# A decode layer on one core: half of the query's weights loaded first, w2 in six pieces, x and the result in four transfers each

## The chip, the cores and the metric

The kernel runs on one core of one Trainium2 chip. The metric is the device time in microseconds (us) of one execution, as the median of several. TensorE is called PE, VectorE DVE, ScalarE ACT, GpSimd POOL, and SyncE SP. SP computes nothing here: it only issues transfers. ACT issues a few as well.

## What is computed

One token for each of four sequences (B = 4, D = 1024) goes through an attention block with a sliding window over a cache and then through a gated feed-forward block, each with a layer norm ahead and a residual sum behind. The weights and the caches are bf16.

```python
x  = A_x                                              # [4, 1, 1024]
q  = layernorm(x) @ wq                                # wq [1024, 4096]: 32 heads of 128
k, v = k_cache[:, :, -2048:, :], v_cache[:, :, -2048:, :]   # 4 kv heads, 8 query heads to each
o  = softmax(q @ k.T * 128**-0.5) @ v
h  = x + o @ wo                                       # wo [4096, 1024]
n  = layernorm(h)
out = h + (silu(n @ w1) * (n @ w3)) @ w2              # w1, w3 [1024, 3584]; w2 [3584, 1024]
```

## The kernel before

**The ring of loads.** Everything large passes through five slots of 128 partitions x 16384 bf16 (4 MB each), in the order of the list `ring`: the K cache in two slots of two sequences each (`k`), the first half of wq, two slots without a load that hold the transposed K (`kT`), the second half of wq, V in two slots, wo in two, w1 in two, w3 in two, w2 in two. `fill()` walks the list. It takes a slot and issues its load on SP (L133), and it stops at an entry whose slot is still held; `done(name, i)`, called in the program behind the last reader of a part, goes on with it. So all large loads stand in one queue, SP's, in the ring's order, and what can hold a load back is the release of a slot by PE.

**w2 in pieces.** w2 lies as 28 rows of 1024 values in each of the 128 partitions, 256 KB for one row over all partitions. `W2B = [16, 8, 2, 2]` cuts the rows into four transfers; the first fills one slot, the other three share the next. PE takes four matmuls for a row (L491, `y2_ps`), and it waits at the head of each piece for that piece.

**x and the result.** The 4 x 1024 values of x are laid into the tile `x_nat` [128, 256] as four quarters of 256 columns: quarter c of sequence b goes to partition 32c + 8b (`S = 8`), the other partitions are zero. This is one transfer of 16 rows of 512 bytes, issued by ACT (L149). The layer norm (`layernorm_T`) reads every eighth column of the transposed tile and writes every eighth of `n_T`, and PE's operand of 32 columns has its four live ones there. The result lies the same way in `res`, and leaves in two transfers of eight rows each, one from SP (L503) and one from ACT (L504).

**The order of the work.** The order on each engine is that of the program (`manual_schedule`). PE: the sums of the first layer norm (L198); 256 transposes of K (L241), which DVE and ACT copy into `kT` by turns (L243, L245); 64 matmuls of the query (L259), 32 for each half of wq; then for each sequence the scores, the softmax and the output (L294 to L386); the projection with wo (L434); w1 and w3 (L458); w2 (L491). DVE adds the residual to the last sum (L501), and the result is sent.

**Completion.** A transfer signals its end on one of eight semaphores, which are given out in turn to all transfers, of SP and ACT alike. A transfer that takes a semaphore again waits at its issue for the one that had it before.

Of the kernel before, what the change touches and what calls it, by code (L numbers as in the profile page):

```python
# [10 lines left out]
P = 128  # L11
ACT = mybir.ActivationFunctionType
ALU = mybir.AluOpType
AX = mybir.AxisListType
BF16 = mybir.dt.bfloat16
FP32 = mybir.dt.float32
# [7 lines left out]
def kernel(  # L24
# [20 lines left out]
    nc = tc.nc  # L45

    B, _, D = A_x.shape
    Hkv, Sk, Dh = A_k_cache.shape[1], A_k_cache.shape[2], A_k_cache.shape[3]
    NQ = A_wq.shape[1]
    Hq = NQ // Dh  # L50
    REP = Hq // Hkv
    W = min(4096, max(256, Sk // 4))
    F = B_w1.shape[1]
    KC = D // P
    FC = F // P
    NK = W // P
    C = 4
    R = 32
    S = R // B
    DQ = D // C  # L60
    FQ = F // C
    FH = FQ // 2
# [5 lines left out]
    x_flat = A_x.flatten_outer_dims()  # L68
    out_flat = out.flatten_outer_dims()
# [7 lines left out]
    w1_v = B_w1.rearrange("(p kc) f -> p kc f", kc=KC)  # L77
    w3_v = B_w3.rearrange("(p kc) f -> p kc f", kc=KC)
# [7 lines left out]
    ps = ctx.enter_context(tc.tile_pool(name="ps", bufs=1, space=bass.MemoryType.PSUM))  # L86
# [3 lines left out]
    def of_cache(cache, b):  # L90
        return cache[b, :, Sk - W : Sk, :].rearrange("g (i j) d -> i g (j d)", j=JR)

    def pair(parts):
        return [parts[0:2], parts[2:4]]

    k_, v_ = (
        pair([(name, b, [JR, Dh], of_cache(cache, b)) for b in range(B)])
        for name, cache in (("k", A_k_cache), ("v", A_v_cache))
    )
    kT_ = pair([("kT", b, [JR, P], None) for b in range(B)])  # L100
    wo_ = pair([("wo", g, [1, T * D], wo_v[:, g : g + 1, :]) for g in range(Hkv)])

    def four_rows(name, view, n):
        return [[(name, i, [4, n], view[:, 4 * i : 4 * i + 4, :])] for i in range(KC // 4)]

    wq_ = four_rows("wq", wq_v, NQ)
    ring = k_ + wq_[:1] + kT_ + wq_[1:] + v_ + wo_ + four_rows("w1", w1_v, F) + four_rows("w3", w3_v, F)
    W2B = [16, 8, 2, 2]
    w2_ = []
    f0 = 0  # L110
    for i, n in enumerate(W2B):
        w2_.append(("w2", i, [n, D], w2_v[:, f0 : f0 + n, :]))
        f0 += n
    ring += [w2_[:1], w2_[1:]]
    views = {}
    taken = []
    used = set()
# [19 lines left out]
    def get(name, i):  # L137
        return views[(name, i)]

    def done(name, i):  # L140
        used.add((name, i))
        fill()
# [3 lines left out]

    x_nat = act.tile([P, DQ], BF16)
    nc.vector.memset(x_nat[:], 0.0)
    nc.scalar.dma_start(out=x_nat[::S, :], in_=x_flat.rearrange("b (c n) -> c b n", c=C))  # L149
    fill()  # L150

    ident = const.tile([P, P], BF16)
# [8 lines left out]
        out=t32[:], in_=ident[:].rearrange("p (q h) -> p h q", q=C), axis=AX.X, op=ALU.add  # L161
# [4 lines left out]
    for q in range(C):  # L166
# [3 lines left out]
        out=negm[:], in_=t32[:].rearrange("p (g r) -> p g r", g=Hkv), axis=AX.X, op=ALU.add  # L170
    )
    nc.vector.tensor_scalar(
        out=negm[:], in0=negm[:], scalar1=-1.0, scalar2=-NEG, op0=ALU.add, op1=ALU.mult
# [3 lines left out]
        out=jmask[:, :, 0], in_=ident[:].rearrange("p (j h) -> p j h", j=JM), axis=AX.X, op=ALU.add  # L177
# [6 lines left out]
    for l in range(2):  # L184
        nc.gpsimd.tensor_copy(
            out=strip[:, l, B - 1 :].rearrange("p (c x) -> p c x", c=C)[:, :, : B * Hkv].rearrange(
                "p c (g b) -> p c g b", b=B
            )[:, :, :, 0],
            in_=t32[:].rearrange("p (g c l) -> p l c g", g=Hkv, c=C)[:, l],
        )  # L190

    def layernorm_T(h_T, tag):

        both = act.tile([P, 2, KC, B], FP32, tag=tag + "_both")
        nc.vector.tensor_copy(out=both[:, 0], in_=h_T[:, :, ::S])
        nc.vector.tensor_tensor(out=both[:, 1], in0=both[:, 0], in1=both[:, 0], op=ALU.mult)  # L196
        sums_ps = ps.tile([P, 2, KC, B], FP32, tag="kt3")
        nc.tensor.matmul(sums_ps[:], lhsT=ones_f[:], rhs=both[:], start=True, stop=True)  # L198
        sums = act.tile([P, 2, B], FP32, tag=tag + "_sums")
        nc.vector.tensor_reduce(  # L200
            out=sums[:], in_=sums_ps[:].rearrange("p t k b -> p t b k"), axis=AX.X, op=ALU.add
        )
        mean = act.tile([P, 2, B], FP32, tag=tag + "_mean")
        nc.vector.tensor_single_scalar(out=mean[:], in_=sums[:], scalar=1.0 / D, op=ALU.mult)
        rstd = act.tile([P, 1, B], FP32, tag=tag + "_rstd")
        nc.vector.tensor_tensor(out=rstd[:, 0], in0=mean[:, 0], in1=mean[:, 0], op=ALU.mult)
        nc.vector.tensor_tensor(out=rstd[:, 0], in0=mean[:, 1], in1=rstd[:, 0], op=ALU.subtract)  # L207
        nc.scalar.activation(  # L208
            out=rstd[:, 0], in_=rstd[:, 0], func=ACT.Sqrt, bias=eps_t[:], scale=1.0
        )  # L210
        nc.vector.reciprocal(out=rstd[:, 0], in_=rstd[:, 0])
        n_T = act.tile([P, KC, R], BF16, tag=tag + "_nT")
        nc.gpsimd.memset(n_T[:], 0.0)
        hc = act.tile([P, KC, B], FP32, tag=tag + "_hc")
        nc.vector.tensor_tensor(
            out=hc[:], in0=both[:, 0], in1=mean[:, 0:1, :].to_broadcast([P, KC, B]), op=ALU.subtract
        )
        nc.vector.tensor_tensor(
            out=n_T[:, :, ::S], in0=hc[:], in1=rstd[:].to_broadcast([P, KC, B]), op=ALU.mult
        )  # L220
        return n_T

    def transpose_quads(dst, src, n):

        nc.vector.transpose(
            out=dst.rearrange("p j r -> p (j r)"), in_=src.rearrange("p (q j) -> p j q", j=n)
        )

    x_T = act.tile([P, KC, R], BF16)
    transpose_quads(x_T[:], x_nat[:], KC)  # L230
    xn_T = layernorm_T(x_T[:], "ln1")


    n_step = 0
# [11 lines left out]
            n_step += 1  # L246
        done("k", b)


    q_ps = [ps.tile([P, REP // 2, Dh], FP32, tag=f"sc{hf}", name=f"q_ps{hf}") for hf in range(2)]  # L250
    HALF = REP // 2
    for i in range(KC // 4):
        w = get("wq", i)
        for kk in range(4):
            kc = 4 * i + kk
            for hf in range(2):
                for c in range(C):
                    o = (2 * c + hf) * HALF * Dh
                    nc.tensor.matmul(  # L259
                        q_ps[hf][R * c : R * c + R],  # L260
                        lhsT=xn_T[:, kc, :],
                        rhs=w[:, kk, o : o + HALF * Dh],
                        start=(kc == 0),
                        stop=(kc == KC - 1),
                        tile_position=(0, R * c),
                    )
        done("wq", i)
    q_sb = act.tile([P, REP, Dh], BF16)
    nc.vector.tensor_copy(out=q_sb[:, :HALF], in_=q_ps[0][:])  # L269
    nc.scalar.copy(out=q_sb[:, HALF:], in_=q_ps[1][:])  # L270
    qT_ps = ps.tile([P, REP, Hkv, R], BF16, tag="kt0")
# [6 lines left out]
    for b in range(B):  # L278
        nc.vector.tensor_copy(  # L279
            out=Qm[:, b].rearrange("p (g y) -> p g y", y=QW)[:, :, :REP],  # L280
            in_=qT_ps[:, :, :, S * b].rearrange("p r g -> p g r"),
        )


# [122 lines left out]
    for l in range(2):  # L407
        for b in range(B):
            nc.tensor.matmul(  # L409
                on_ps[:, l],  # L410
                lhsT=strip[:, l, B - 1 - b : B - 1 - b + P],
                rhs=om[:, b],
                start=(b == 0),
                stop=(b == B - 1),
# [5 lines left out]
    oP = act.tile([P, Hkv, T, R], BF16)  # L420
    nc.gpsimd.memset(oP[:], 0.0)
    nc.vector.tensor_copy(  # L422
        out=oP[:, :, :, ::S],
        in_=oX[:, :, : Hkv * B].rearrange("p t (g b) -> p g t b", b=B),
    )

# [2 lines left out]
    for g in range(Hkv):  # L429
        w = get("wo", g)  # L430
        for t in range(T):
            for c in range(C):
                o = t * D + c * DQ
                nc.tensor.matmul(  # L434
                    y_ps[R * c : R * c + R, :],
                    lhsT=oP[:, g, t, :],
                    rhs=w[:, 0, o : o + DQ],
                    start=(g == 0 and t == 0),
                    stop=(g == Hkv - 1 and t == T - 1),
                    tile_position=(0, R * c),  # L440
# [4 lines left out]
    h_T = act.tile([P, KC, R], FP32)  # L445
    transpose_quads(h_T[:], h1[:], KC)
    hn_T = layernorm_T(h_T[:], "ln2")


# [36 lines left out]
    fc = 0  # L486
    for i, n in enumerate(W2B):
        w = get("w2", i)
        for ff in range(n):
            for c in range(C):  # L490
                nc.tensor.matmul(  # L491
                    y2_ps[R * c : R * c + R, :],
                    lhsT=hg_T[:, fc, :],
                    rhs=w[:, ff, c * DQ : (c + 1) * DQ],
                    start=(fc == 0),
                    stop=(fc == FC - 1),
                    tile_position=(0, R * c),
                )
            fc += 1
    res = act.tile([P, DQ], BF16)  # L500
    nc.vector.tensor_tensor(out=res[:], in0=y2_ps[:], in1=h1[:], op=ALU.add)  # L501
    out_v = out_flat.rearrange("b (c n) -> c b n", c=C)
    nc.sync.dma_start(out=out_v[: C // 2], in_=res[: P // 2 : S, :])  # L503
    nc.scalar.dma_start(out=out_v[C // 2 :], in_=res[P // 2 :: S, :])  # L504


# [28 lines left out]
```

## Time and profile before

| | us |
|---|---|
| median of 3 runs (lowest to highest) | 140.11 (139.94 to 140.18) |
| the profiled execution | 140.13 |
| its span in the profile | 138.3 |
| time outside the span | 1.8 |

| engine | busy us | share of the span |
|---|---|---|
| PE | 80.2 | 58% |
| DVE | 52.9 | 38% |
| ACT | 42.7 | 31% |
| queue q1 (SP's loads): 55.58 MB | | 94.4% of 16 DMA engines |

The page gives busy shares in 40 slices of the span, the DMA engines' rate beside them, and the chain of waits that ended last. The timeline lists instructions in order of time, merged, with the idle time of the engine ahead of them in brackets and what ended it; a line of a transfer in it shows the issue on the queue (SPq, ACTq), not the data. Every time below is counted from the start of the span.

### The profile page before, as it was taken

The numbers are of one execution on the slowest core, as the hardware profiler recorded it, in microseconds if no ns is written. First come the engines' busy times: TensorE is split into PE (matmuls) and PEld (weight loads), VectorE is DVE, ScalarE is ACT, GpSimd is POOL, SyncE is SP. The second block draws the span as 40 slices with busy tenths as digits, with TensorE's granted clock in tenths as the row PEclk, the third lists the DMA queues.
The fourth block names the chain that finished last, engine by engine and source line by source line (L and its number), as shares of the span: only waits on it lengthen the run. The fifth ranks groups of instructions, "written<-read, shape, count | busy, mean of one in ns | idle before, by whom it ended". The sixth has DMA issues, their size and how long they took to land.

```text
span 138.3 us, 2012 instructions
## 1 busy us (share of the span) xinstructions
PE 80.2 (58%) x866; PEld 47.5 (34%) x868; DVE 52.9 (38%) x97; ACT 42.7 (31%) x57; POOL 4.2 (3%) x18
## 2 busy tenths in 40 slices
PE   0029898921903889328918998659539901703780
PEld 0029887820301322014304434537324400202550
DVE  3036676520000235177087197540330298350001
ACT  3005988850000325998807900000040200000000
POOL 7400000000000000000000000000000000000000
PEclk9999999998555799975797799965865896555555
DMA  4999999999989999999999999999999999999930
GB/s 152 399 423 431 431 436 455 455 441 398 445 384 426 441 417 417 450 407 431 450 400 431 433 469 431 394 448 448 419 398 448 456 411 430 445 407 398 406 148 2
DMA packets 3217, 55.72 MB, mean 403 GB/s; under 512 B 360, under 2 KB 392, under 8 KB 648
## 3 DMA queue, kind: packets, MB, share of 16 engines
q1 hardware_dynamic: 3178, 55.58, 94.4%
q8 instruction: 7, 0.11, 0.3%
q10 hardware_dynamic: 30, 0.01, 0.0%
q14 instruction: 2, 0.02, 0.0%
HBM read 55.58 MB, written 0.01 MB: 402 GB/s over the span
## 4 chain that ended last, share of the span: by engine, by line
DMA 49%; PE 27%; DVE 13%; ACT 4%; SPq 3%; issue 2%; DVEq 0%
DMA s_wq<-in_A_wq_dram 29%; DMA s_w<-in_B_w_dram 20%; PE o_ps L369 10%; PE y_ps L434 5%; ACT P L334 4%; PE sc_ps L294 3%; DVE PT L346 3%; SPq L133 3%; PE gu_ps L458 2%; PE q_ps L259 2%; DVE om L386 2%; DVE od L378 2%; PE on_ps L409 1%; PE tot_ps L355 1%; PE nm_ps L323 1%
## 5 line engine op out<-in xcount | busy, mean ns | idle before, releaser
L334 ACT ACTIVATE P<-sc_ps,bias 128x512 bf16<-128x512 f32 x16 | 19.7, 1417 | 9.6 <-DVE bias L331 9.6
L241 PE MATMUL kt_ps<-ident,s_k 128*128 128x128 bf16 x256 | 17.3, 228 | 1.3 <-ACT s_kT L245 1.0
L369 PE MATMUL o_ps<-s_v,PT 128*128 128x512 bf16 x62 | 17.5, 439 | 0.3 <-issue 0.2
L241 PEld LDWEIGHTS <-s_k 128*128 128x128 bf16 x256 | 16.3, 103 | 2.3 <-issue 1.7
L245 ACT COPY s_kT<-kt_ps 128x1024 bf16<-128x1024 bf16 x16 | 15.7, 1012 | 2.5 <-PE kt_ps L241 2.5
L458 PE MATMUL gu_ps<-s_w,n_T 128*32 128x448 bf16 x128 | 10.7, 513 | 8.8 <-DMA s_w<-in_B_w_dram 6.8
L259 PE MATMUL q_ps<-s_wq,n_T 128*32 128x512 bf16 x64 | 7.0, 615 | 11.8 <-DMA s_wq<-in_A_wq_dram 11.8
L243 DVE COPY s_kT<-kt_ps 128x1024 bf16<-128x1024 bf16 x16 | 11.1, 693 | 5.8 <-PE kt_ps L241 5.8
L491 PE MATMUL y_ps<-s_w,hg_T 128*32 128x256 bf16 x112 | 6.6, 418 | 8.0 <-DMA s_w<-in_B_w_dram 8.0
L369 PEld LDWEIGHTS <-PT 128*128 128x128 bf16 x64 | 7.2, 117 | 9.2 <-issue 4.4
L346 DVE STREAM_TRANSPOSE PT<-P 128x2048 bf16<-128x2048 bf16 x4 | 9.2, 2303 | 2.7 <-ACT P L334 2.7
L208 ACT ACTIVATE rstd<-rstd,eps_t 128x4 f32<-128x4 f32 x2 | 0.6, 297 | 29.5 <-DVE rstd L207 29.5
L458 PEld LDWEIGHTS <-n_T 128*32 128x32 bf16 x128 | 4.7, 131 | 14.1 <-issue 11.6
L294 PE MATMUL sc_ps<-s_kT,Qm 128*32 128x512 bf16 x64 | 8.5, 603 | 0.4 <-DVE Qm L279 0.4
L491 PEld LDWEIGHTS <-hg_T 128*32 128x32 bf16 x112 | 4.9, 142 | 10.0 <-issue 5.9
L259 PEld LDWEIGHTS <-n_T 128*32 128x32 bf16 x64 | 2.7, 137 | 15.6 <-issue 15.5
L269 DVE CAST q_sb<-q_ps 128x512 bf16<-128x512 f32 x1 | 0.7, 692 | 18.3 <-PE q_ps L259 18.3
L198 PE MATMUL sums_ps<-both,ones_f 128*128 128x64 f32 x4 | 1.1, 373 | 11.2 <-DVE both L196 11.2
L434 PE MATMUL y_ps<-s_wo,oP 128*32 128x256 bf16 x128 | 6.5, 397 | 1.7 <-DVE oP L422 1.7
L378 DVE SCALAR_TENSOR_TENSOR od<-o_ps,rinv,jmask 128x512 f32<-128x512 f32 x4 | 3.0, 751 | 8.4 <-PE o_ps L369 8.3
L270 ACT CAST q_sb<-q_ps 128x512 bf16<-128x512 f32 x1 | 0.6, 585 | 17.8 <-PE q_ps L259 17.8
L310 PE MATMUL mx_ps<-ident_f,rmax 128*1 128x128 f32 x8 | 1.7, 302 | 7.4 <-DVE rmax L308 7.4
(68 smaller groups left out, 64.7 us busy)
## 6 DMA issues: line engine op xcount, KB each, us to landing
s_w<-in_B_w_dram SPq DMA_DIRECT2D x4, 3584.0 KB, 21.2
s_k<-in_A_k_cache_dram SPq DMA_DIRECT2D x4, 2048.0 KB, 16.1
s_wq<-in_A_wq_dram SPq DMA_DIRECT2D x2, 4096.0 KB, 35.3
s_v<-in_A_v_cache_dram SPq DMA_DIRECT2D x4, 2048.0 KB, 25.1
s_wo<-in_A_wo_dram SPq DMA_DIRECT2D x4, 2048.0 KB, 25.5
s_w<-in_B_w_dram SPq DMA_DIRECT2D x1, 4096.0 KB, 28.0
s_w<-in_B_w_dram SPq DMA_DIRECT2D x1, 2048.0 KB, 25.7
s_w<-in_B_w_dram SPq DMA_DIRECT2D x2, 512.0 KB, 27.0
```

Of the source, the lines that this page charges most:

```text
L241: nc.tensor.transpose(out=kt_ps[:, jj], in_=k[:, jb * JB + jj, :], identity=ident[:])
L243: nc.vector.tensor_copy(out=kT[:, jb * JB : (jb + 1) * JB], in_=kt_ps[:])
L245: nc.scalar.copy(out=kT[:, jb * JB : (jb + 1) * JB], in_=kt_ps[:])
L259: nc.tensor.matmul(q_ps[hf][R * c : R * c + R], lhsT=xn_T[:, kc, :], rhs=w[:, kk, o : o + HALF * Dh], start=(kc == 0), stop=(kc == KC - 1) ...
L294: nc.tensor.matmul(sc_ps[b][R * q : R * q + R], lhsT=Qm[:, b, g * R : (g + 1) * R], rhs=v[:, g, q], start=(g == 0), stop=(g == Hkv - 1), t ...
L334: nc.scalar.activation(out=P4[:, :, :, g], in_=sc_ps[b][:].rearrange("p (j i) -> p j i", i=L5), func=ACT.Exp, bias=bias[:, g : g + 1], sca ...
L346: nc.vector.transpose(out=PT[:].rearrange("p j h -> p (j h)"), in_=stage.pop(("P4", b))[:].rearrange("p j i g -> p (j i g)"),)
L369: nc.tensor.matmul(o_ps[:], lhsT=PT[:, i * JM : (i + 1) * JM, :].rearrange("p j h -> p (j h)"), rhs=v[:, i * JM : (i + 1) * JM, :], start= ...
L378: nc.vector.scalar_tensor_tensor(out=od[:], in0=o_ps[:], scalar=rinv[:, 0:1], in1=jmask[:].to_broadcast([P, JM, Dh]), op0=ALU.mult, op1=AL ...
L434: nc.tensor.matmul(y_ps[R * c : R * c + R, :], lhsT=oP[:, g, t, :], rhs=w[:, 0, o : o + DQ], start=(g == 0 and t == 0), stop=(g == Hkv - 1 ...
L458: nc.tensor.matmul(out_ps[hf][R * c : R * c + R], lhsT=hn_T[:, kc, :], rhs=w[:, kk, o : o + FH], start=(kc == 0), stop=(kc == KC - 1), til ...
L491: nc.tensor.matmul(y2_ps[R * c : R * c + R, :], lhsT=hg_T[:, fc, :], rhs=w[:, ff, c * DQ : (c + 1) * DQ], start=(fc == 0), stop=(fc == FC ...
```

## The change

The ring begins with the first half of wq and the K cache follows it; the matmuls of that half are moved in PE's program ahead of the transposes of K, and those of the second half stay behind them. w2 is cut in 7, 6, 8, 4, 2 and 1 rows, the first two in one slot, the other four in the next. Quarter c of sequence b now lies in partition 32c + b, so x arrives in four transfers of four consecutive partitions, all issued by ACT, and the result leaves in four: two from SP, two from ACT. Every tile that followed the stride of eight follows the new places (`:B` for `::S`).

```diff
-    ring = k_ + wq_[:1] + kT_ + wq_[1:] + v_ + wo_ + ...
-    W2B = [16, 8, 2, 2]
+    ring = wq_[:1] + k_ + kT_ + wq_[1:] + v_ + wo_ + ...
+    W2B = [7, 6, 8, 4, 2, 1]
...
-    ring += [w2_[:1], w2_[1:]]
+    ring += [w2_[:2], w2_[2:]]
...
-    nc.scalar.dma_start(out=x_nat[::S, :], in_=x_flat.rearrange("b (c n) -> c b n", c=C))
+    for c in range(C):
+        nc.scalar.dma_start(out=x_nat[R * c : R * c + B, :], in_=x_flat[:, c * DQ : (c + 1) * DQ])
     fill()
...
-        nc.vector.tensor_copy(out=both[:, 0], in_=h_T[:, :, ::S])
+        nc.vector.tensor_copy(out=both[:, 0], in_=h_T[:, :, :B])
...
-            out=n_T[:, :, ::S], in0=hc[:], in1=rstd[:].to_broadcast([P, KC, B]), op=ALU.mult
+            out=n_T[:, :, :B], in0=hc[:], in1=rstd[:].to_broadcast([P, KC, B]), op=ALU.mult
...
+    query(0)                      # the 32 matmuls of the first half of wq
     for b in range(B):            # the transposes of K, unchanged
...
+    query(1)                      # the 32 matmuls of the second half
...
-            in_=qT_ps[:, :, :, S * b].rearrange("p r g -> p g r"),
+            in_=qT_ps[:, :, :, b].rearrange("p r g -> p g r"),
...
-        out=oP[:, :, :, ::S],
+        out=oP[:, :, :, :B],
...
-    out_v = out_flat.rearrange("b (c n) -> c b n", c=C)
-    nc.sync.dma_start(out=out_v[: C // 2], in_=res[: P // 2 : S, :])
-    nc.scalar.dma_start(out=out_v[C // 2 :], in_=res[P // 2 :: S, :])
+    for i in range(2):
+        for half, eng in enumerate((nc.sync, nc.scalar)):
+            c = 2 * half + i
+            eng.dma_start(
+                out=out_flat[:, c * DQ : (c + 1) * DQ], in_=res[R * c : R * c + B, :]
+            )
```

More of the change, by code (lines that the diff above doesn't have):

```diff
@@ L58 @@
     R = 32
-    S = R // B
     DQ = D // C
@@ L106 @@
     wq_ = four_rows("wq", wq_v, NQ)
-    ring = k_ + wq_[:1] + kT_ + wq_[1:] + v_ + wo_ + four_rows("w1", w1_v, F) + four_rows("w3", w3_v, F)
-    W2B = [16, 8, 2, 2]
+    ring = wq_[:1] + k_ + kT_ + wq_[1:] + v_ + wo_ + four_rows("w1", w1_v, F) + four_rows("w3", w3_v, F)
+    W2B = [7, 6, 8, 4, 2, 1]
     w2_ = []
@@ L231, with query @@
     xn_T = layernorm_T(x_T[:], "ln1")
-    n_step = 0
-    for b in range(B):
-        k = get("k", b)
-        kT = get("kT", b)
-        for jb in range(JR // JB):
-            kt_ps = ps.tile([P, JB, P], BF16, tag=f"kt{n_step % 3}")
-            for jj in range(JB):
-                nc.tensor.transpose(out=kt_ps[:, jj], in_=k[:, jb * JB + jj, :], identity=ident[:])
-            if n_step % 2 == 0:
-                nc.vector.tensor_copy(out=kT[:, jb * JB : (jb + 1) * JB], in_=kt_ps[:])
-            else:
-                nc.scalar.copy(out=kT[:, jb * JB : (jb + 1) * JB], in_=kt_ps[:])
-            n_step += 1
-        done("k", b)
     q_ps = [ps.tile([P, REP // 2, Dh], FP32, tag=f"sc{hf}", name=f"q_ps{hf}") for hf in range(2)]
     HALF = REP // 2
-    for i in range(KC // 4):
+    def query(i):
         w = get("wq", i)
@@ L267 @@
         done("wq", i)
+    query(0)
+    n_step = 0
+    for b in range(B):
+        k = get("k", b)
+        kT = get("kT", b)
+        for jb in range(JR // JB):
+            kt_ps = ps.tile([P, JB, P], BF16, tag=f"kt{n_step % 3}")
+            for jj in range(JB):
+                nc.tensor.transpose(out=kt_ps[:, jj], in_=k[:, jb * JB + jj, :], identity=ident[:])
+            if n_step % 2 == 0:
+                nc.vector.tensor_copy(out=kT[:, jb * JB : (jb + 1) * JB], in_=kt_ps[:])
+            else:
+                nc.scalar.copy(out=kT[:, jb * JB : (jb + 1) * JB], in_=kt_ps[:])
+            n_step += 1
+        done("k", b)
+    query(1)
     q_sb = act.tile([P, REP, Dh], BF16)
```

## The prediction

> **What bounds the kernel now.** I read the page's slices first, then its chain.
>
> ```profile
> DMA  4999999999989999999999999999999999999930
> GB/s 152 399 423 431 431 436 455 455 441 398 445 384 426 441 417 417 450 407 431 450 400 431 433 469 431 394 448 448 419 398 448 456 411 430 445 407 398 406 148 2
> ...
> DMA 49%; PE 27%; DVE 13%; ACT 4%; SPq 3%; issue 2%; DVEq 0%
> ```
>
> The 16 DMA engines are at nine tenths or more from the second slice to the 37th, with one eight. 55.58 MB at some 430 GB/s is 129 us of the 138.3. The chain does name PE and DVE for 40%, but only because it walks back from one load's issue through the slot that let it go; the engines' row shows that the data never ran dry meanwhile. So the kernel is one stream of loads with a head and a tail, and an edit counts if it moves the first packet, the bytes' rate, the tail, or lets the queue run empty.
>
> The timeline of the last 12 us is the tail:
>
> ```profile
> 126.88 3.61 PE L491 MATMUL y_ps<-s_w,hg_T 128*32 128x256 bf16 x64 [6.53 <-DMA s_w<-in_B_w_dram]
> ...
> 131.77 2.33 PE L491 MATMUL y_ps<-s_w,hg_T 128*32 128x256 bf16 x40 [1.28 <-DMA s_w<-in_B_w_dram]
> ...
> 134.30 0.62 PE L491 MATMUL y_ps<-s_w,hg_T 128*32 128x256 bf16 x8 [0.20 <-DMA s_w<-in_B_w_dram]
> ...
> 134.97 0.42 DVE L501 TENSOR_TENSOR res<-y_ps,h 128x256 bf16<-128x256 f32 x1 [12.06 <-PE y_ps L491]
> 135.42 0.66 SPq L503 DMA_DIRECT2D out_dram<-res  x1
> 135.42 0.60 ACTq L504 DMA_DIRECT2D out_dram<-res  x1
> ```
>
> PE waits for each piece of w2: the 16 rows at 126.88, the next 8 at 131.77, the last two at 134.30. Eight matmuls, the sum and the result's way out follow. By the records of SP, its wait for the result ends at 137.43, 1.35 after its issue ends at 136.08; two further waits of 0.06 and the closing steps of all engines lead to 138.3.
>
> The timeline of the start, with the SP queue's and ACT's first issues and the end of the query:
>
> ```profile
> 0.73 2.59 SPq L133 DMA_DIRECT2D s_k<-in_A_k_cache_dram  x4
> ...
> 1.03 1.19 ACTq L149 DMA_DIRECT2D x_nat<-in_A_x_dram  x1
> ...
> 3.36 1.14 SPq L133 DMA_DIRECT2D s_wq<-in_A_wq_dram  x2
> ...
> 8.37 0.62 DVE L225 STREAM_TRANSPOSE x_T<-x_nat 128x256 bf16<-128x256 bf16 x1 [6.03 <-DMA x_nat<-in_A_x_dram]
> ...
> 28.54 10.44 SPq L133 DMA_DIRECT2D s_v<-in_A_v_cache_dram  x4
> 34.15 3.60 PE L259 MATMUL q_ps<-s_wq,n_T 128*32 128x512 bf16 x32 [5.64 <-DMA s_wq<-in_A_wq_dram]
> ...
> 43.86 3.40 PE L259 MATMUL q_ps<-s_wq,n_T 128*32 128x512 bf16 x32 [6.11 <-DMA s_wq<-in_A_wq_dram]
> ```
>
> **The new order at the start** is worth nothing in itself: either way 16.8 MB must land before the last 32 query matmuls, and half of them are already done then. What changes is PE's order, so I follow what PE now waits for. x: its 16 rows go in between the packets of the big loads; the packet records show them at 5.59, 6.22, 6.93 and 7.56 on four DMA engines, one behind each 16 KB packet of K (0.61 us), the first after five of those. Behind 32 KB packets (1.22 us) I expect the first near 8.7 and the last near 12.4; that the four issues on ACT take longer than the one of 1.19 is inside this, and ACT has nothing else queued but a table load. From x's transpose to `n_T` takes 8.37 to 12.09, 3.7 us, so n_T is ready near 16.7, behind the 4 MB of wq (two K loads had landed at 13.2). The 32 matmuls take 3.4 to 3.6: 20.3. Then 64 transposes for each sequence at some 4.5 us, behind K's landings at 18.1, 24.3, 29 and 34.1: done at about 38.7. The second half of wq lands at 43.8, so PE has 5 us in hand and the rest of PE's program starts as before.
>
> Queues it is moved past: on SP, K now stands behind wq, and the stream is the same length. The four x transfers use up completion semaphores, so in the built program the fourth K load waits for the first wq load (about 13.2) and the second wq load for the first x; three K loads are queued then, enough until about 27. V's first load needs two sequences transposed, near 29 (28.54 before), and its second pair all four, near 38.7 (37.79); at both times the queue holds more than 5 us. Later issues come 12 us or more ahead of need: the last of w1's loads is issued at 79.16, when the data ahead of it lasts until 91.6. DVE's edits of stride (0.20 to 0.46 us each) hide there too. Cost: 0; if the cover goes, one us for each us of an empty queue.
>
> The head: the first issue, of K, takes 0.65 and the first packet moves at 2.16. The wq issues at the same stage take 0.63 and 0.47, and later weights 0.33, so the gain lies between 0 and 0.33. I take **-0.1**, by the nearest rows, those of wq.
>
> **w2 in six pieces.** Two pieces more, each 8 packets for a DMA engine. From 126.88 to 131.77 eight rows in one piece took 4.89, or 0.611 a row; from 131.77 to 134.30 four rows in two pieces took 2.53, or 0.633. That is 0.06 per added piece. The packet records say 161 ns for 4 KB and 614 for 16 KB, so a packet has some 10 ns that don't scale, 0.08 a piece. Two pieces: 0.11 to 0.19 (no gain is possible, the bytes are the same); I take **+0.15**. PE's side: four matmuls a row at 58 ns each (2.33 us for 40), 0.23, against 0.61 for the row's data, so PE has caught up at the last row.
>
> The Trainium skill speaks against this: "DMA: Bandwidth & Descriptors", section on bandwidth, advises batches of 1 MiB or more and gives 341 GB/s for 1 MB against 425 for 16 MB. By an estimate from that, the 1.8 MB of the last three pieces would take 5.4 us instead of 4.3, and the sum would be 1 us longer. The trace disagrees as far as it goes: its two 0.5 MB pieces, issued long ahead, came at 414 GB/s.
>
> **The last matmuls.** Eight become four. One takes 0.37 to 0.42, four run side by side, and eight took 0.62; four need some 0.40, so **-0.2** (between -0.15 and 4 x 58 ns = -0.23).
>
> **The result.** Two issues in a row on each queue where there was one. No trace row has a transfer of four rows. Issues of 128 regular rows take 0.33 alone; those of 8 rows here 0.66 and 0.60; that of 16 rows (x) 1.19. A line through the last two gives 0.3 to 0.4 for four rows. I take 0.40: 2 x 0.40 + 0.06 between them - 0.66 = +0.20. Bounds: 2 x 0.33 + 0.05 - 0.66 = +0.05, and 2 x 0.66 + 0.06 - 0.66 = +0.72. The write itself: eight packets stood in two chains of four, 0.12 from first to last; four consecutive partitions against four rows should use four engines with one packet each, -0.09. The closing waits: the last transfer's semaphore is now the last in SP's list, so up to 0.12 of the two waits behind it lies ahead; half, -0.06. Together **+0.05** (-0.16 to +0.72).
>
> The same page, in the section on why a completion counts 16, states that a transfer uses the largest number of engines up to 16 that divides the outer size on both sides. The rows agree for the old shapes (16 against 4: four engines; 8 against 2: two). By it the new ones use four; no row shows that yet.
>
> **Sum:** -0.1 + 0.15 - 0.2 + 0.05 = -0.1. From the profiled execution's 140.13, which is the median of 140.11 within 0.02, that gives 140.0. All low ends: -0.33 + 0.11 - 0.23 - 0.16 = -0.6; all high ends: 0 + 0.19 - 0.15 + 0.72 = +0.8. One more unknown has no term: the 16 engines land a piece up to 2 us apart (132.24 to 134.26 for the last), since a few were held up by 16 KB fetches of instructions of about 1 us, and the end waits for the slowest. Another start may draw this by 0.3 either way.
>
> **Rivals.**
> 1. *Head and spread pay.* The first issue costs 0.33, the result's issues 0.33, and the slow engines come 0.3 earlier: 139.4 to 139.7. For: all later weight issues of wq's form cost 0.33. Against: the first ones cost 0.47 and 0.63.
> 2. *The result's second issue costs full price (slower).* At 0.6 to 0.66 each, the second transfer ends 0.6 to 0.7 later; with the rest, 140.45. It decides above 0.5 per issue. For: eight rows cost no less than 128 rows did, so the price may not follow the rows. Against: x, with twice the rows, cost twice.
> 3. *x comes late and blocks PE (slower).* PE's transposes now stand behind the query, which stands behind the layer norm. Up to a query that ends at 26 nothing moves; if V's first load can't be issued before 43.8, the queue runs dry, which needs the query to end past 35, x past 27. Then each us costs a us: 141 to 144. For: x is interleaved with packets of twice the length. Against: it has four packets per engine, and wq only eight.
>
> **How the numbers follow.** What a measurement of this kernel can tell from no change is 0.2%, 0.28 us. The forecast, 139.75 to 140.4, has 0.44: 0.09 of it faster, 0.32 same, 0.03 slower. Rival 1 has 0.27 (0.24 faster, 0.03 same), rival 2 has 0.25 (0.05 same, 0.20 slower), rival 3 has 0.04. So faster 0.33, same 0.40, slower 0.27. The range 139.4 to 140.8 leaves out rival 3 and the outer ends of the others.
>
> **What would show it.** Right: DMA slices at nine to the end, the first packet near 2.05, x's transpose near 13, the second query matmuls at 43 to 44, one wait of PE for each w2 piece and the last block of four matmuls at 0.4, each result issue near 0.4. Wrong: a slice of seven or less between 20 and 50 us (rival 3), result issues at 0.6 (rival 2), a last w2 landing earlier or later than 134.2 by more than 0.4 (the spread).

## The result and the profile after

The changed kernel takes 139.38 us (139.21 to 139.47, 6 runs) where the kernel before takes 139.98 (139.88 to 140.18, 6 runs beside it): a ratio of 0.9954, interval 0.9941 to 0.9967. It is faster by 0.6 us. The forecast was 140.0 in a range of 139.4 to 140.8: the stream and its cover went as told, and the head and the way of the result out were both priced too dear.

The page's slices and chain of the changed kernel:

```profile
DMA  5998999999899999999999999999999999999950
GB/s 152 458 459 382 429 434 434 415 438 505 376 410 429 415 438 419 434 429 415 443 417 429 422 467 425 438 417 434 425 430 425 425 447 388 414 437 431 400 219 2
...
DMA 51%; PE 28%; DVE 13%; ACT 4%; issue 2%; SPq 1%; DVEq 0%
```

The stream is as full as before; no slice runs dry. The timeline of its last 14 us:

```profile
124.80 1.47 PE L496 MATMUL y_ps<-s_w,hg_T 128*32 128x256 bf16 x24 [1.06 <-DMA s_w<-in_B_w_dram]
...
129.69 1.90 PE L496 MATMUL y_ps<-s_w,hg_T 128*32 128x256 bf16 x32 [3.43 <-DMA s_w<-in_B_w_dram]
...
132.19 1.04 PE L496 MATMUL y_ps<-s_w,hg_T 128*32 128x256 bf16 x16 [0.60 <-DMA s_w<-in_B_w_dram]
...
133.42 1.05 PE L496 MATMUL y_ps<-s_w,hg_T 128*32 128x256 bf16 x12 [0.18 <-DMA s_w<-in_B_w_dram]
...
134.52 0.42 DVE L506 TENSOR_TENSOR res<-y_ps,h 128x256 bf16<-128x256 f32 x1 [11.96 <-PE y_ps L496]
134.97 0.67 SPq L510 DMA_DIRECT2D out_dram<-res  x2
134.98 0.62 ACTq L510 DMA_DIRECT2D out_dram<-res  x2
```

PE finds each piece of w2 just landed and is done with it before the next; the line with 12 matmuls is the last two pieces, of two rows and of one. The last two lines hold the surprise: two issues on each queue now take 0.67 and 0.62 together, as long as one took before. The rows by tile say it for each issue (ns, smallest, median and largest; before it was 664 on SP and 599 on ACT):

```profile
L510 SPq DMA_DIRECT2D out_dram<-res x2: 274/311/348, 135.0 to 135.4; - x2
L510 ACTq DMA_DIRECT2D out_dram<-res x2: 275/292/308, 135.0 to 135.3; - x2
```

At the start, the first load's issue takes 0.65 before and 0.41 after (a line of the chain of waits before, and one of the timeline after):

```profile
0.73 0.65 SPq L133
```

```profile
0.73 0.41 SPq L132 DMA_DIRECT2D s_wq<-in_A_wq_dram  x1
```

The windows give the bytes by the time at which their packets begin (the last column is GB/s). Before, nothing moves ahead of 2.0:

```profile
1.50:2.00 0.50, 0.00 (x0) 0.00 (x0) 0.43 (x3) 0.00 (x0) 0.39 (x3) 1.00 0.00 0
2.00:2.50 0.50, 0.00 (x0) 0.00 (x0) 0.34 (x3) 0.25 (x1) 0.50 (x4) 1.00 1.83 524
```

After, three quarters of the 16 engines' first packets have begun by then:

```profile
1.50:2.00 0.50, 0.00 (x0) 0.00 (x0) 0.43 (x3) 0.00 (x0) 0.39 (x3) 1.00 2.82 786
2.00:2.50 0.50, 0.00 (x0) 0.00 (x0) 0.34 (x3) 0.00 (x0) 0.50 (x4) 1.00 0.84 262
```

Cut into stretches by the packet and instruction records, the two profiled executions (140.13 and 139.33) compare so:

| stretch | before | after | difference |
|---|---|---|---|
| start to the first packet | 2.16 | 1.77 | -0.39 |
| first packet to the last of w2 | 131.62 | 131.82 | +0.20 |
| to the start of the last sum | 1.19 | 0.93 | -0.26 |
| to the result's first issue | 0.45 | 0.45 | 0 |
| to the end of the span | 2.93 | 2.57 | -0.36 |

These sum to -0.8; the medians say -0.6. Two profiled executions of the changed kernel differ by 0.27 in the end of the stream alone (133.59, and 133.86 in a later run), so a single pair of profiles tells the short stretches well and the long one only to some 0.2 or 0.3.

### The profile page after: what moved, and what is told of

The parts are those of the page before. It is cut to its first block, busy times and chain, and to the rows that moved or that the text cites. A ratio compares the mean times of both kernels' runs of the same rounds, so it can differ in the third digit from the quotient of the medians.

```text
span 137.5 us, 2022 instructions
## 1 busy us (share of the span) xinstructions
PE 78.7 (57%) x866; PEld 45.4 (33%) x868; DVE 52.6 (38%) x97; ACT 42.7 (31%) x57; POOL 4.2 (3%) x18
## 4 chain that ended last, share of the span: by engine, by line
DMA 51%; PE 28%; DVE 13%; ACT 4%; issue 2%; SPq 1%; DVEq 0%
DMA s_wq<-in_A_wq_dram 31%; DMA s_w<-in_B_w_dram 20%; PE o_ps L374 11%; ACT P L339 4%; PE y_ps L439 4%; PE sc_ps L299 3%; DVE PT L351 3%; PE q_ps L244 2%; DVE om L391 2%; PE gu_ps L463 2%; DVE od L383 2%; PE tot_ps L360 1%; PE nm_ps L328 1%; PE on_ps L414 1%; SPq L132 1%
## 5 line engine op out<-in xcount | busy, mean ns | idle before, releaser
L374 PE MATMUL o_ps<-s_v,PT 128*128 128x512 bf16 x62 | 18.4, 457 | 0.3 <-issue 0.2
L264 PE MATMUL kt_ps<-ident,s_k 128*128 128x128 bf16 x256 | 16.1, 219 | 1.1 <-ACT s_kT L268 1.0
L264 PEld LDWEIGHTS <-s_k 128*128 128x128 bf16 x256 | 15.0, 98 | 2.9 <-issue 2.5
L463 PE MATMUL gu_ps<-s_w,n_T 128*32 128x448 bf16 x128 | 9.8, 474 | 9.8 <-DMA s_w<-in_B_w_dram 8.0
L244 PE MATMUL q_ps<-s_wq,n_T 128*32 128x512 bf16 x64 | 7.2, 630 | 7.4 <-DMA s_wq<-in_A_wq_dram 5.6
L463 PEld LDWEIGHTS <-n_T 128*32 128x32 bf16 x128 | 4.4, 122 | 14.5 <-issue 11.5
L496 PEld LDWEIGHTS <-hg_T 128*32 128x32 bf16 x112 | 4.2, 124 | 10.8 <-issue 6.8
L198 PEld LDWEIGHTS sums_ps<-both,ones_f 128*128 128x128 f32 x4 | 0.8, 250 | 16.4 <-DVE both L196 16.4
L244 PEld LDWEIGHTS <-n_T 128*32 128x32 bf16 x64 | 2.4, 139 | 10.8 <-issue 8.6
L479 DVE RECIPROCAL eg<-eg 128x896 f32<-128x896 f32 x1 | 5.8, 5753 | 0.0
L439 PE MATMUL y_ps<-s_wo,oP 128*32 128x256 bf16 x128 | 4.9, 326 | 1.5 <-DVE oP L427 1.5
```

The source lines that it names most:

```text
L244: nc.tensor.matmul(q_ps[hf][R * c : R * c + R], lhsT=xn_T[:, kc, :], rhs=w[:, kk, o : o + HALF * Dh], start=(kc == 0), stop=(kc == KC - 1) ...
L264: nc.tensor.transpose(out=kt_ps[:, jj], in_=k[:, jb * JB + jj, :], identity=ident[:])
L374: nc.tensor.matmul(o_ps[:], lhsT=PT[:, i * JM : (i + 1) * JM, :].rearrange("p j h -> p (j h)"), rhs=v[:, i * JM : (i + 1) * JM, :], start= ...
L439: nc.tensor.matmul(y_ps[R * c : R * c + R, :], lhsT=oP[:, g, t, :], rhs=w[:, 0, o : o + DQ], start=(g == 0 and t == 0), stop=(g == Hkv - 1 ...
L463: nc.tensor.matmul(out_ps[hf][R * c : R * c + R], lhsT=hn_T[:, kc, :], rhs=w[:, kk, o : o + FH], start=(kc == 0), stop=(kc == KC - 1), til ...
L479: nc.vector.reciprocal(out=eg[:], in_=eg[:])
```

## The experiments

In the expectations a transfer is "flat" when its rows follow one step on both sides, in memory and over the partitions, and "nested" when one side needs two steps, as K's loads do (32 groups of 4 rows for the 128 partitions).

**The three parts alone, and the order without PE's part.** e1_order takes the ring's and PE's new order alone:

```diff
-    ring = k_ + wq_[:1] + kT_ + ...
+    ring = wq_[:1] + k_ + kT_ + ...        # and query(0) ahead of the transposes
```

> The kernel before, with the new ring order and PE's new order alone (w2 in 16, 8, 2, 2; x and result as before). Theory A (flat pattern): a load whose rows follow one step on both sides, as wq's, is issued in 0.41 and moves data from 1.77, where K's nested one takes 0.65 and 2.16; the whole stream comes 0.35 to 0.4 earlier: 139.6. Rival B (all of the gain is in the result): no change, 140.0. Rival C (the start pays, but through PE's order): 139.6 too, and the ring order alone does not.

Measured: 139.84 against 140.01, ratio 0.9985 (0.9976 to 0.9993). The first packet is at 1.73, as early as in the changed kernel, but only half of that reaches the end. So there is a gain, against rival B, and it is smaller than the 0.35 to 0.4 that was expected.

e4_ring keeps PE's order:

```diff
-    query(0)                    # ahead of the transposes
...
-    query(1)
+    query(0)
+    query(1)                    # both behind them
```

> As e1, but PE keeps its order: the transposes of K first, then all 64 query matmuls. Theory A: the same as e1, 139.6, since only the first issue counts and PE has room. Rival C (PE's order): 140.0, and e1 is faster by 0.3 or more.

Measured: 139.78 as the median and a ratio of 0.9999 (0.9983 to 1.0016). Two of its eleven runs took 140.66 and 140.69, the other nine 139.72 to 139.94; why the two are longer is open, and with them the interval is too wide to tell e1 from no gain. The profile tells more: first packet at 1.73, last of w2 at 133.44 (133.46 in e1). By that one profile PE's order is worth nothing that shows, as the prediction had it.

e2_pieces takes w2's pieces alone:

```diff
-    W2B = [16, 8, 2, 2]
+    W2B = [7, 6, 8, 4, 2, 1]    # two in one slot, four in the next
```

> The kernel before, with w2 in 7, 6, 8, 4, 2, 1 alone. By the prediction's terms +0.15 for two more pieces and -0.2 for four matmuls fewer behind the last: 139.95, within 0.1 of before. Rival (a fixed price of each small transfer): 140.5 to 141.

Measured: 140.11 against 140.01, ratio 1.0005 (0.9996 to 1.0014): no gain. In its profile the stretch to the last sum is 0.93 instead of 1.19, so the four matmuls are saved; but from the result's first issue to the end takes 3.06 instead of 2.93. That loss has nothing to do with w2; e13 comes back to it. The profiled execution, of 139.82, is the shortest of e2's runs, so its longer stretches say little of the median.

e3_layout takes the places of x and of the result alone:

```diff
-    nc.scalar.dma_start(out=x_nat[::S, :], ...)
+    for c in range(C):          # and the result likewise, two on SP, two on ACT
+        nc.scalar.dma_start(out=x_nat[R * c : R * c + B, :], ...)
```

> The kernel before, with x and the result in four transfers of four consecutive partitions alone. Theory A (flat pattern): two issues of 0.3 in the place of one of 0.6, and the data moves 0.8 after the first issue instead of 1.2 to 1.5, so the span from the result's first issue to the end is 2.55 instead of 2.93: 139.6. Rival (the prediction's own term, second issue on top): 140.0 to 140.1, and the gain seen comes from the other parts.

Measured: 139.83 against 140.01, ratio 0.9986 (0.9977 to 0.9995). From the result's first issue to the end takes 2.69, 0.24 less than before; its issues are 274 to 352 ns. The second issue on each queue does not come on top. The stretch misses the expected 2.55 by 0.14, which e13 explains too. e12_pieces_layout adds w2's pieces to this, K still first:

> The changed kernel with the old order of the first loads and of PE: K first. If the parts add up, it lacks only the order's share, 0.2: 139.6. Rival (the order has a larger share when the rest is in place, since the three parts alone summed to 0.3 and the whole to 0.6): 139.8 or more.

Measured: 139.68 against 139.97, ratio 0.9977 (0.9967 to 0.9986). The order, which it lacks, is worth about 0.3 by that.

**What makes an issue short.** In e5_res4_strided the result leaves in four transfers of four rows, as in the change, but from the old places, eight partitions apart:

```diff
+            eng.dma_start(out=out_flat[:, c * DQ : (c + 1) * DQ],
+                          in_=res[R * c : R * (c + 1) : S, :])
```

> The kernel before, with the result in four transfers but on the old partitions: each carries one quarter, four partitions eight apart, one step on both sides; x as before. Theory A (flat pattern): the same gain as with consecutive partitions, 0.3 to 0.4, issues of 0.3: 139.6. Rival D (consecutive partitions are what pays): issues near 0.6 each, 140.0 or up to 140.5.

Measured: 140.97 against 140.11, ratio 1.0061 (1.0047 to 1.0075). Theory A alone falls here: the same four rows to the same addresses, and 0.86 us slower than before. Of its stretch behind the first issue, 3.88 instead of 2.93, the last data packet has 0.82; the other 0.13 is SP's closing list, of which more below. The rows by tile:

```profile
L505 SPq DMA_DIRECT2D out_dram<-res x2: 742/750/757, 135.3 to 136.1; - x2
L505 ACTq DMA_DIRECT2D out_dram<-res x2: 588/628/668, 135.3 to 136.0; - x2
```

Each issue costs twice what it costs from neighbouring partitions, and as much as the old one with eight rows, or more. The number of rows is not what is paid for.

Is it then neighbouring partitions, whatever else? e10_res8 holds the live columns of the even quarters in rows 28 to 31 as well, so that eight result rows lie side by side, and sends them in one transfer for each queue. On the memory's side that is a nested pattern, two quarters of four sequences:

```diff
+    out_v = out_flat.rearrange("b (c n) -> c b n", c=C)
+    nc.sync.dma_start(out=out_v[: C // 2], in_=res[R - B : R + B, :])
+    nc.scalar.dma_start(out=out_v[C // 2 :], in_=res[3 * R - B : 3 * R + B, :])
```

> The changed kernel, with the result in two transfers of eight consecutive partitions: the live columns of the even quarters are held in rows 28 to 31 as well, so that the result of quarters 0 and 1 lies in partitions 28 to 35, and that of 2 and 3 in 92 to 99. Three small DVE instructions more in each layer norm and one behind the output, beside loads. Theory D (neighbouring partitions make an issue short, whatever the rows): one issue of 0.35 for each queue, the second pair of issues gone, 0.2 to 0.35 less than the changed kernel: 139.1. Rival (the nested pattern on the memory side costs 0.6, as it does for 8 spread rows): 139.4 to 139.5.

Measured: 139.94, ratio 0.9998 (0.9990 to 1.0007): the gain of the change is gone. From the first issue to the end takes 3.10 instead of 2.57. By the records 0.29 of that is the data's way out and 0.19 the closing list (three waits behind the last transfer, where the changed kernel has none), which nobody had meant to move.

```profile
L514 SPq DMA_DIRECT2D out_dram<-res x1: 777/777/777, 135.0 to 135.0; - x1
L515 ACTq DMA_DIRECT2D out_dram<-res x1: 730/730/730, 135.0 to 135.0; - x1
```

Eight neighbouring partitions with a nested pattern cost as much as spread ones. So either departure makes an issue long, and of the shapes run here only rows that follow one step in memory from partitions side by side make it short. In e10 rows and nesting change together, and no run sends eight such rows with one step; at the head, e9 below parts the two with 128 rows. The data follow suit. From the first result issue to the end of the last data packet takes 1.66 before, 1.30 in e3, 1.31 in the changed kernel, 2.48 in e5 and 1.60 in e10, by the packet records. e11_res8_13 is e10 with one piece of w2 fewer, and stands at 139.86:

> As e10, with w2 in 13, 8, 4, 2, 1. By the price of a piece 0.0 to 0.1 less than e10.

That agrees with a price too small to be measured. The same cut in the changed kernel itself, e7_13 (`W2B = [13, 8, 4, 2, 1]`):

> The changed kernel with w2 in 13, 8, 4, 2, 1: one piece fewer, at a place where PE has nothing late to catch up. By the price of a piece, 0.08 less than the changed kernel: 139.3. Rival (the early pieces let PE start on w2 earlier, and that counts): slower than the changed kernel by 0.1 or more.

Measured: 139.41, ratio 0.9949 (0.9936 to 0.9961), not to be told from the changed kernel. Its expected 0.08 is below what such runs resolve, and it has one closing wait more behind the last transfer, 0.06.

e8_x4_strided sends only x in four transfers, on the old places:

> The kernel before, with x in four transfers on the old partitions, the result as before. Theory A and the prediction: no change in time, 140.0, since x is not on the path; issues of 0.3 to 0.6 on ACT. Rival (x's issues disturb the first loads): a first landing of K later than 8.4 and 140.1 to 140.3.

Measured: 140.10 against 140.11, ratio 1.0000 (0.9991 to 1.0009). Its issues on ACT take 588 to 1194 ns, against 265 to 617 in the changed kernel; neither is on the path. But they answer the line that the prediction drew through two transfers. Before, x's 16 rows went out in one issue, here in four of four rows each:

```profile
L149 ACTq DMA_DIRECT2D x_nat<-in_A_x_dram x1: 1192/1192/1192, 1.0 to 1.0; - x1
```

```profile
L150 ACTq DMA_DIRECT2D x_nat<-in_A_x_dram x4: 588/662/1194, 1.0 to 3.6; - x4
```

By the records the 1194 is the first of the four, with a quarter of the rows. So 1.19 is what ACT's first issue from spread places took at the start, beside SP's first loads, and not the price of 16 rows; the three behind it, of 588 to 673, cost what eight rows cost at the end. What makes the first one longer is not shown.

**The head.** e6_first_16k splits the first load of the changed kernel into two of two rows each, so its packets are of 16 KB:

```diff
+                    for r in (0, 2):
+                        nc.sync.dma_start(out=view[:, r : r + 2], in_=src[:, r : r + 2])
```

> The changed kernel, with the first half of wq loaded in two transfers of two rows, so its packets are 16 KB as K's are and its pattern stays flat. Theory A: first packet at 1.77 as in the changed kernel, the time 139.4 and at most 0.15 more. Rival E (larger packets start earlier): first packet near 2.1, 139.7.

Measured: 139.49, ratio 0.9958 (0.9944 to 0.9971), first packet at 1.76. The packet's length does not matter for the head; its 0.1 over the changed kernel agrees with two closing waits behind the last transfer. e9_wq_nested reads the first load from wq in a nested order:

```diff
+    wq_n = A_wq.rearrange("(g i kc) n -> i g (kc n)", g=4, kc=KC)
```

> The changed kernel, with the first load taken from the same bytes of wq in a nested order, as K's loads are: 32 groups of 4 rows for the 128 partitions, each row still 32 KB. It changes which row of wq lies in which partition, so the query is another one. Theory A for the head (a nested source costs 0.25 in the issue and more behind it): issue near 0.65, first packet near 2.15, as in the kernel before. Rival (what pays is that wq is not K, or that it is the longer row): issue 0.41, first packet 1.77.

Its issue takes 0.63 and its first packet starts at 2.14, and its windows look like those of the kernel before, though it loads wq:

```profile
0.73 0.63 SPq L133 DMA_DIRECT2D s_wq<-in_A_wq_dram  x1
```

```profile
1.50:2.00 0.50, 0.00 (x0) 0.00 (x0) 0.43 (x3) 0.00 (x0) 0.39 (x3) 1.00 0.01 2
2.00:2.50 0.50, 0.00 (x0) 0.00 (x0) 0.35 (x3) 0.00 (x0) 0.50 (x4) 1.00 3.18 920
```

So the head gains because wq's rows follow one step and K's don't. That this gain reaches the end is not shown by e9: its single run, 139.49, lies within the runs of the changed kernel (139.21 to 139.68, with e15's).

**The part that the parts did not have.** The ratios of e1, e2 and e3 alone multiply to 0.9976; the whole has 0.9954, 0.3 us more; with some 0.0009 to 0.0013 of uncertainty on each of the four ratios, that is little beyond the noise. In the traces the kernels differ in one thing that nobody chose: which of the eight semaphores the result's transfers draw. SP ends with a fixed list of five waits. Before, and in e1 and e3, its wait for the last transfer is the third and two follow; in e2 the first, and four follow; in the changed kernel, and in e12, the last. e13_lanes3 and e14_lanes1 shift this by three and by one spare transfer, issued by ACT behind the query:

```diff
+    for i in range(3):          # 1 in e14
+        nc.scalar.dma_start(out=spare[:B, i * 64 : (i + 1) * 64], in_=x_flat[:, :64])
```

> The changed kernel with three more transfers of four short rows into a spare tile, issued by ACT behind the query, where nothing waits for them. They move every later transfer by three of the eight completion semaphores, so the last transfer of the result comes early in SP's closing list instead of last. Theory L (the closing waits behind it cost 0.06 each and explain why the parts alone sum to less than the whole): 0.15 to 0.25 slower than the changed kernel, 139.6. Rival (the missing part lies elsewhere): as the changed kernel within 0.1.

> As e13 with one such transfer: the last transfer of the result stands third of five in the closing list. Theory L: two waits, 0.1 slower than the changed kernel, 139.5. Rival: no difference.

> The changed kernel itself, beside e13 and e14 on the same chip, as what they are compared with: 139.4 by every theory.

Measured: 139.86, 139.69 and 139.42, with ratios of 0.9990 (0.9982 to 0.9999), 0.9980 (0.9971 to 0.9989) and 0.9958 (0.9944 to 0.9972). SP's own waits show how long its closing list stood at the result in one wait, for the changed kernel, for e14 and for e13 in this order:

```profile
SPq L538 <- DMA out_dram<-res: 0.4, 1, 0.4
```

```profile
SPq L541 <- DMA out_dram<-res: 0.9, 1, 0.9
```

```profile
SPq L541 <- DMA out_dram<-res: 1.1, 1, 1.1
```

The longer that one stand, the more of the list is still to come: by SP's records no wait, two and four follow the last transfer's. From the result's first issue to the end takes 2.57 in the changed kernel (2.55 in e15), 2.67 in e14 and 2.79 in e13, so each wait behind the last transfer costs 0.06. Two more in e2 and two fewer in the whole make 0.26 of the 0.3 that the parts did not have, and e12, which draws as the whole does, is below the product of e2 and e3 by 0.2. The waits account for 0.1 and 0.22 of what e14 and e13 lost (0.27 and 0.44, more than theory L's 0.1 and 0.15 to 0.25); the rest lies ahead of the result and within what single profiles vary, and stays open.

## Why the prediction was wrong, point by point

**The result's issues: the step that failed.** It had 2 x 0.40 + 0.06 - 0.66 = +0.20 for them and +0.05 with the rest, with a price that follows the rows, from a line through two transfers (16 rows 1.19, 8 rows 0.6 to 0.66). Both were spread over partitions and nested in memory, and the new ones are neither; and e8 shows that the 1.19 was not a price of rows. They cost 0.27 to 0.35, so two cost no more than one had, 0.62 to 0.67, and the data moved 0.76 after the first issue instead of 1.24. The kernel's end came 0.24 earlier behind the first issue in e3, where the list's draw is as before; the prediction had +0.11 for that, its +0.05 without the closing waits. The term for the write, -0.09, did not come: the last data packet to the last count on its semaphore takes 0.43 in the changed kernel, 0.33 before. "0.33 for 128 regular rows" was the nearest row after all: it was of the same form, and it was used as a bound only. e5 shows how near the other outcome was: with spread rows, rival 2's mechanism is right, each issue at full price, and worse than rival 2 had it.

**The head: the mechanism right, the term too small.** -0.1 was taken, from issues of wq that stood behind others (0.63 and 0.47), with -0.33 as the end. The first issue took 0.41, and the first packet came 0.62 behind its end instead of 0.77, which no term had; together -0.39, outside the bound. e9 shows that both belong to the pattern. Of this -0.39 the order is worth -0.2 to -0.3 at the end (e1, and e12 against the changed kernel); that it is the head which saves this is argued, since e9's one run does not show the loss.

**The closing waits.** Half of 0.12 was taken. The last transfer is indeed last in the list: two waits of 0.06 less than before, 0.12, as e13 and e14 bear out. It is also part of why w2's pieces alone gained nothing: there the draw went the other way, by 0.12.

**w2's pieces.** The price of +0.15 is not measured. With wq first the stream's last packet came at 133.44 and 133.46 with the old pieces (e4, e1) and at 133.57 to 133.86 with the six (the changed kernel, e6, e10, e15); with K first it came at 133.53 to 133.82 with the old pieces (before, e3, e5, e8) and at 133.60 and 133.72 with the six (e2, e12). Taken for the four matmuls: -0.2; the stretch says -0.26. By the Trainium skill's table ("DMA: Bandwidth & Descriptors", section on bandwidth) the prediction had estimated a loss of 1 us for the small pieces; it did not come, as the interval of e2's ratio ends at 1.0014. That table is of transfers issued by GpSimd, and these go out from SP behind others.

**The stream and its cover: right.** The transpose of x starts at 13.35 ("near 13"), the query's first half at 17.00, the transposes of K end at 37.8 (38.7 was reckoned), and the second half starts at 43.39 ("43 to 44"), when the load lands:

```profile
13.35 0.63 DVE L225 STREAM_TRANSPOSE x_T<-x_nat 128x256 bf16<-128x256 bf16 x1 [11.01 <-DMA x_nat<-in_A_x_dram]
...
17.00 3.60 PE L244 MATMUL q_ps<-s_wq,n_T 128*32 128x512 bf16 x32 [1.83 <-DVE n_T L218]
```

```profile
35.79 2.00 PE L264 MATMUL kt_ps<-ident,s_k 128*128 128x128 bf16 x32 [0.16 <-ACT s_kT L268]
43.39 3.60 PE L244 MATMUL q_ps<-s_wq,n_T 128*32 128x512 bf16 x32 [5.60 <-DMA s_wq<-in_A_wq_dram]
```

The bracket of the last line is PE's 5 us in hand. The fourth K load waits at its issue until 13.07 for the first wq load, as told, and costs nothing. x's first packet came at 4.95 and not near 8.7, its last at 12.48 (12.4 was reckoned). V's first load was reckoned near 29, behind two sequences; it went out at 20.65, behind the query's first half (`PE q_ps L244` in SP's waits), which only adds to the cover. The page's row of nine tenths reaches the 38th slice, not the 37th. Rival 3 did not come up.

**Engines per transfer.** The Trainium skill's rule ("DMA: Bandwidth & Descriptors", on why a completion counts 16), by which four rows against four go over four engines, agrees with the new shapes: in the packet records each result transfer of four rows is four packets with four completions, where each of eight rows before had two completions.

**The range.** Its low end, 139.4, took the head's far end (-0.33) and the result's (-0.16) together, and both lay too near: the profiles say -0.39 and -0.36. The stream's +0.20 took part of that back, so the time fell only 0.02 below the range. That is in part luck, and so is the level: the sum started from 140.13, and the kernel before took 139.98 beside the changed one. Rival 1 came out in its two prices, a short first issue and short result issues, and in its time. Of its third condition, slow engines 0.3 earlier, little shows: the last piece lands over 1.88 us, 2.02 before, by the semaphore records. It had 0.27 because the nearest rows by time were preferred to the nearest by form.

## What to carry to other kernels

Price an issue by its pattern, not by its rows or bytes: find a row of the trace whose transfer has the same form on both sides, one step in memory and partitions side by side, and take that, even if it moves a thousand times more. In a kernel that is one stream of loads, look at the pattern of the first load and of the last store, since these two issues alone stand open on both ends. And before parts of a change are judged one by one for some 0.1%, see whether they moved something that none of them is about, here the draw of completion semaphores.

## What was not expected of the hardware

- A result issue of four rows from partitions side by side took 0.27 to 0.35; with the partitions eight apart 0.59 to 0.76; with eight rows side by side but nested in memory 0.73 to 0.78. The data started 0.75 to 0.84 after such a short issue began, and 1.24 to 1.67 after a long one.
- A first load started its data 1.00 to 1.04 after its issue began with one step in memory, and 1.41 to 1.45 with a nested source, whether it was K or wq and whether packets had 16 or 32 KB.
- Each of SP's waits in the closing list took 0.06 even when what it waited for was long done.
